# Attention's keys transposed four chunks at a time: 112-row tiles in place of 48-row pieces, and two weight buffers in place of three

## The chip, the cores and the metric

The kernel runs on one core of one Trainium2 chip. The metric is the device time of one execution in microseconds (us). A core has a matrix engine (PE, with its weight loads listed apart as PEld), three engines for elementwise work (DVE, ACT, POOL) and a queue engine (SP) that issues the DMAs. Each engine works through its own list of instructions in order. PE reads SBUF and writes PSUM, which has eight banks.

## What is computed

Three layers, one after the other, in fp32 (B = 4, H = 8, S = 768, D = 48; 3072 tokens of 384 channels):

```python
for t in range(S):                       # attention: a gated linear recurrence per head
    state = alpha[:, :, t, :, None] * state + np.einsum('bhd,bhe->bhde', k[:, :, t], v[:, :, t])
    y[:, :, t] = np.einsum('bhd,bhde->bhe', q[:, :, t], state)
...
P = np.exp(logits)                       # mixture of 8 experts: 8 rounds of row and column scaling
...
for e in range(E):
    out += P[:, e:e + 1] * (np.maximum(x @ w1[e], 0.0) @ w2[e])
...
h = x @ w_in                             # last layer
g = h * np.cos(h)
return (g @ w_out).astype(np.float32)
```

## The kernel before

**Matrix products.** Each fp32 operand of the large products is split into a high and a low part of type fp32r, and a product is made of three (high by high, high by low, low by high). The weights come in passes: 8 experts and 2 halves of the last layer. A pass has 8 weight pieces `w{c}{i}` (chunk c = 0 to 3; i = 0 into the hidden layer, i = 1 out of it), each with a high tile `w..h` and a low tile `w..l`. A piece is loaded into a staging buffer `raw`, cast on ACT into `w..h`, and POOL writes the remainder to `w..l`; only then may the buffer take the next load (`Weights.prep`, `Weights.load`). There are `NRAW` staging buffers. The tiles of one pass are overwritten for the next while the last block of the pass runs.

**Stage 1** holds attention and the first expert, side by side. The tokens are cut into 12 units of 256, and a unit's heads into 4 pairs, so attention has 48 slots (unit, pair). In a slot (`attention`, the loop over `slots`):

- `ew`, two slots ahead: scans and products on DVE, ACT and POOL that make the decayed q, k and the tile `k6` (the keys, decayed to the end of their chunk of 64 tokens). A pair's two heads lie in partitions 0 to 47 and 64 to 111.
- PE transposes `k6` chunk by chunk into PSUM bank 0, and ACT copies it to `kt`. Call this group kT. Per chunk it is one `transpose` for the head at 64 to 111 and one `matmul` with the identity for the head at 0 to 47; in the trace the matmul counts twice, so four chunks are 12 PE instructions `bank<-ident,acc` with 48 rows.
- PE multiplies keys and queries (`pg`, 48 rows by 64), and values with `kt` (`pk`, 64 rows by 48); DVE carries the state over the chunks; PE makes the output (`py`, 128 rows by 48) one slot later, and ACT copies it to `x`.

As soon as a unit's 4 pairs are done, the first expert's block of that unit can run (`Passes.block`): per hidden tile 9 products of `w.0` and 9 of `w.1`, all 128 rows by 128 columns with 256 tokens moving. These are called R below, the name of no tile. After attention, `sinkhorn` scales the gates, and stage 2 runs passes 1 to 9 in blocks of 512 tokens.

**What sets the order.** A `Plan` records all instructions and issues them by a list scheduler: every instruction has a rank (attention 0, products 1, `ew` and weight preparation 1 or 2), a planned cost and planned waits, and each engine takes the lowest rank among what is ready. The planned cost of a PE instruction with up to 64 columns differs from that of a wider one, so a change of shape changes the order.

**Memory.** `late` are the last 1024 columns of the output accumulator `acc`, unused until attention ends; `k6` (three tiles) and `qka` (q, k and alpha as loaded, four tiles) lie there and in `fbuf`.

Of the kernel before, what the change touches and what calls it, by code (L numbers as in the profile page):

```python
# [9 lines left out]
F32 = mybir.dt.float32  # L10
# [9 lines left out]
B, H, S, D = 4, 8, 768, 48  # L20
# [5 lines left out]
CH = 64  # L26
# [4 lines left out]
UN = 256  # L31
# [3 lines left out]
AMIN, AMAX = 0.25, 1.0  # L35
LAG = 2
LAG3 = 3
NRAW = 3
FARENA, RARENA = 9232, 10240
SEG = 32  # L40
SCAN = (SEG + 1) * (UN // SEG)
DBG = None
# [15 lines left out]
def vw(t, off, dims, p0=0, p1=128):  # L58
    a = t[p0:p1]
    return bass.AP(a.tensor, a.offset + off, [list(a.ap[0])] + [list(d) for d in dims])  # L60
# [130 lines left out]
class Arena:  # L191
# [17 lines left out]
    def ring(self, n, shape, dtype):  # L209
        return ring([self.tile(shape, dtype) for i in range(n)])  # L210
# [8 lines left out]
class Weights:  # L219
# [7 lines left out]
    def load(self):  # L227
        if self.loaded == len(self.order):
            return
        p, c, i = key = self.order[self.loaded]  # L230
        r = self.raw[key] = self.k.raw[self.loaded % NRAW]
        self.loaded += 1
# [79 lines left out]
class Kernel:  # L312
    def __init__(self, tc, ctx, qka, vv, nat, vt, wts, w8, wg, cst, out):
# [9 lines left out]
        self.w = [[[const.tile([128, CW], F32R, name=f"w{c}{i}{z}") for z in "hl"] for i in range(2)] for c in range(NCH)]  # L323
        self.raw = [const.tile([128, CW], F32, name=f"raw{i}") for i in range(NRAW)]
        self.ident = const.tile([128, 128], F32, name="ident")
# [61 lines left out]
    def attention(self, pool):  # L387
        e = self.e
        V, A, G, T, SP = e.vector, e.scalar, e.gpsimd, e.tensor, e.sync
        nt0 = UN // CH  # L390
# [9 lines left out]
        m1, m2 = tots()[:, 0:1], tots()[0:1, 0:1]  # L400

        late = [Arena(self.acc[:, k, NTOK - 4 * UN:]) for k in range(KT)]
        qka = ring([z.tile([128, 3, UN], F32) for z in late + [pool]])
        k6s, mask = ring([z.tile([128, UN], F32) for z in late]), self.mask
        pt0, pk = (self.bank[i][:, :nt0 * D].rearrange("p (t d) -> p t d", d=D) for i in (0, 2))
        pg0, py0 = (self.bank[i][:, :UN] for i in (1, 3))
        V.memset(pk, 0.0)
        V.memset(py0, 0.0)
# [10 lines left out]
        def load_v(ui):  # L419
            b, s0, n = UNITS[ui]  # L420
            t = vs[ui % 2]
            for h in range(2):
                r = slice(64 * h, 64 * h + 64)
                SP.dma_start(out=t[r, h], in_=self.vv[b, s0 // UN, r])

        def ew(i):
            t = loaded.pop(i)
            n = UNITS[slots[i][0]][2]
            X, k6, rp, tot, a, f = xt(), k6s(), rps(), tots(), decs(), fwds()
            self.rank(2)  # L430
            state[i] = dict(X=X, k6=k6, qk=t, tot=tot)
            nb, seg = n // 64, [[SEG + 1, n // SEG], [1, SEG]]
            flat = [[SEG, n // SEG], [1, SEG]]

            def tt(eng, o_, a_, b_):
                eng.tensor_tensor(out=o_, in0=a_, in1=b_, op=ALU.mult)

            V.tensor_scalar(vw(a, 1, seg), vw(t, 2 * UN, flat), AMIN, AMAX, op0=ALU.max, op1=ALU.min)

            V.tensor_tensor_scan(out=f[:, :SCAN], data0=a[:, :SCAN], data1=self.heads, initial=0.0, op0=ALU.mult, op1=ALU.add)  # L440
            V.tensor_tensor_scan(out=vw(bwd, SCAN, [[-1, SCAN]]), data0=vw(a, SCAN, [[-1, SCAN]]), data1=self.heads, initial=0.0, op0=ALU.mult, op1=ALU.add)
            tt(G, vw(t, 0, flat), vw(t, 0, flat), vw(f, 1, seg))
            tt(V, vw(t, UN, flat), vw(t, UN, flat), vw(bwd, 2, seg))
            G.tensor_tensor(out=vw(t, 2 * UN, flat), in0=vw(t, 2 * UN, flat), in1=vw(a, 1, seg), op=ALU.subtract)
            first, second = SEG, 2 * SEG + 1
            tt(V, tot[:, :nb], vw(f, first, [[2 * SEG + 2, nb]]), vw(f, second, [[2 * SEG + 2, nb]]))
            tt(V, vw(k6, 0, [[64, nb], [1, 32]]), vw(t, UN, [[64, nb], [1, 32]]), vw(f, second, [[2 * SEG + 2, nb], [0, 32]]))
            A.copy(vw(k6, 32, [[64, nb], [1, 32]]), vw(t, UN + 32, [[64, nb], [1, 32]]))
            V.reciprocal(rp[:, :n // SEG], vw(f, first, [[SEG + 1, n // SEG]]))
            for p0, h in ((0, 1), (64, 0)):  # L450
                p1 = p0 + 64
                tt(V, vw(X, h * UN + 32, [[64, nb], [1, 32]], p0, p1), vw(t, 32, [[64, nb], [1, 32]], p0, p1), vw(f, first, [[2 * SEG + 2, nb], [0, 32]], p0, p1))
                A.copy(vw(X, h * UN, [[64, nb], [1, 32]], p0, p1), vw(t, 0, [[64, nb], [1, 32]], p0, p1))
            a1 = vw(t, 0, [[UN + 32, 2], [64, nb], [1, 32]])
            tt(G, a1, a1, vw(rp, 0, [[1, 2], [2, nb], [0, 32]]))
# [23 lines left out]
        for i in range(len(slots) + 1):  # L479
            if i + 2 < len(slots):  # L480
                ew(i + 2)
            self.rank(0)
            if i < len(slots):
                ui, p = slots[i]
                b, s0, n = UNITS[ui]
                nt = n // CH
                if p == 0 and ui + 1 < len(UNITS):
                    load_v(ui + 1)
                st = state[i]
                t, k6, X, tot = st["qk"], st["k6"], st["X"], st["tot"]  # L490
                pt, pg, kt = pt0[:, :nt], pg0[:, :n], kts()[:, :nt]
                for j in range(nt):
                    T.transpose(pt[0:64, j], k6[64:112, j * CH:(j + 1) * CH], self.ident[64:112, 64:112])
                    T.matmul(pt[64:128, j], k6[0:48, j * CH:(j + 1) * CH], self.ident[0:48, 0:48], start=True, stop=True)
                A.copy(kt, pt)
                yield
                for j in range(nt):
                    js = slice(j * CH, (j + 1) * CH)
                    T.matmul(pg[0:64, js], t[64:112, 1, js], t[64:112, 0, js], start=True, stop=True)
                    T.matmul(pg[64:128, js], t[0:48, 1, js], t[0:48, 0, js], start=True, stop=True)  # L500
                V.copy_predicated(X[0:64, 0, :n], mask[0:64, :n], pg[0:64])
                V.copy_predicated(X[64:128, 1, :n], mask[64:128, :n], pg[64:128])

                self.rank(3)
                d = t[:, 2, :n]
                A.activation(d, d, AF.Square, accum_out=adev[:, i:i + 1])
                if i + 4 < len(slots):
                    loaded[i + 4] = load_qka(*slots[i + 4])
                yield
                self.rank(0)  # L510
                vt, so = vs[ui % 2], sc
                if s0 == 0:
                    G.memset(so[:, p, 0], 0.0)
                for j in range(nt):
                    T.matmul(pk[64:112, j], kt[0:64, j], vt[0:64, 0, p, j], start=True, stop=True)
                    T.matmul(pk[0:48, j], kt[64:128, j], vt[64:128, 1, p, j], start=True, stop=True)
                def step(j):
                    V.scalar_tensor_tensor(out=so[:, p, (j + 1) % nt], in0=so[:, p, j], scalar=tot[:, j:j + 1],
                                           in1=pk[:, j], op0=ALU.mult, op1=ALU.add)

                for j in range(nt - 1):
                    step(j)
                A.copy(vt[64:112, 0, p, :nt], so[64:112, p, :nt])
                A.copy(vt[0:48, 1, p, :nt], so[0:48, p, :nt])
                if s0 + n < S:
                    step(nt - 1)
                yield
            if i > 0:
                ui, p = slots[i - 1]
                b, s0, n = UNITS[ui]  # L530
                nt = n // CH
                X = state.pop(i - 1)["X"]
                vt = vs[ui % 2]
                py = py0[:, :n]
                for j in range(nt):
                    js = slice(j * CH, (j + 1) * CH)
                    T.matmul(py[64:112, js], vt[:, 0, p, j], X[:, 0, js], start=True, stop=True)
                    T.matmul(py[0:48, js], vt[:, 1, p, j], X[:, 1, js], start=True, stop=True)
                t0 = b * S + s0
                if p < 3:  # L540
                    A.copy(self.x[0:48, p, t0:t0 + n], py[0:48])
                    A.copy(self.x[64:112, p, t0:t0 + n], py[64:112])
                else:
                    yt = yts()[:, :n]
                    A.copy(yt, py)
                    self.pieces(yt, t0, n)
                if p == 2:
                    self.done = ui + 1
            yield
# [77 lines left out]
    def stage1(self):  # L627
# [22 lines left out]
        self.rank(2)  # L650
        for _ in range(NRAW):
            w.load()
# [106 lines left out]
    def general(self):  # L759
# [48 lines left out]
        w = self.wq = Weights(self, 0)  # L808
        for _ in range(NRAW):
            w.load()  # L810
# [79 lines left out]
```

## Time and profile before

| what | us |
|---|---|
| median of 3 runs | 2270.36 (2268.06 to 2280.47) |
| the profiled execution, its own time | 2266.68 |
| its span, first to last instruction | 2264.9 |
| PE busy in the span | 2221.3 (98%) |
| DVE, POOL, ACT busy | 1074.9, 815.5, 773.9 |

The profiled execution is 3.7 us under the median, and 1.8 us of its time lie outside the span. PE's busy time is a union of instructions that overlap (a new one starts before the last has drained), so a full PE can still be given less to do; what an instruction costs is read from the distance between starts, not from its duration.

### The profile page before, as it was taken

Reading aid. Unit: us, or ns where it says so; the run is one execution under the profiler, and the core shown is the slowest. Engines: PE = TensorE matmul, PEld = TensorE weight load, DVE = VectorE, ACT = ScalarE, POOL = GpSimd, SP = SyncE. Lnnn points to the kernel's source line nnn. Section 1 sums busy time; section 2 is a strip of 40 time slices with the busy share of each in tenths; the row PEclk is TensorE's granted clock in tenths of the full one; section 3 lists DMA queues with packets and bytes.
Section 4 is the critical chain, followed back from the end, with each engine's and each line's share of the span. In section 5 each row is a group of like instructions: output and inputs, shape, how many; then the busy total and the mean of one; then the engine's idle time right before and its main releaser. Section 6 shows DMA issues by size and latency. Waiting matters only on the chain. (4 is left out here: it accounts for less than half of the span.)

```text
span 2264.9 us, 32287 instructions
## 1 busy us (share of the span) xinstructions
PE 2221.3 (98%) x12790; PEld 1878.9 (83%) x12790; DVE 1074.9 (47%) x2113; ACT 773.9 (34%) x1628; POOL 815.5 (36%) x688
## 2 busy tenths in 40 slices
PE   5999999999999999999999999999999999999998
PEld 4888888978888888888888888888888889998997
DVE  7767667532222333334233423423342237777675
ACT  3444444421122122112212221221222136667664
POOL 5334333243342234224223422422342255447442
PEclk9999999999999999999999999999999999999999
DMA  4211211020011112102111211211120010000000
GB/s 140 80 60 59 68 60 60 10 74 19 19 49 45 31 39 65 29 25 60 47 31 39 65 29 25 61 46 31 40 65 17 5 42 15 1 8 29 29 29 30
DMA packets 70705, 94.89 MB, mean 42 GB/s; under 512 B 6992, under 2 KB 52624, under 8 KB 70544
## 3 DMA queue, kind: packets, MB, share of 16 engines
q1 hardware_dynamic: 70544, 92.74, 13.7%
q8 instruction: 102, 1.67, 0.3%
q14 instruction: 59, 0.48, 0.1%
HBM read 80.42 MB, written 11.11 MB: 40 GB/s over the span
## 5 line engine op out<-in xcount | busy, mean ns | idle before, releaser
L180 DVE SCALAR_TENSOR_TENSOR rbuf<-bank,rbuf 128x512 fp32r<-128x512 f32 (+1 forms) x432 | 271.1, 629 | 822.5 <-ACT rbuf L180 821.6
L180 ACT ACTIVATE rbuf<-bank 128x512 fp32r<-128x512 f32 (+1 forms) x432 | 237.0, 549 | 1021.8 <-PE bank L180 1021.2
L180 POOL TENSOR_TENSOR rbuf<-x,rbuf 128x512 fp32r<-128x512 f32 (+1 forms) x162 | 187.2, 1178 | 716.4 <-ACT rbuf L180 695.8
L180 POOL TENSOR_TENSOR acc<-acc,fbuf 128x512 f32<-128x512 f32 (+1 forms) x252 | 268.4, 1087 | 329.7 <-DVE fbuf L180 239.6
L180 PE MATMUL bank<-rbuf,w11h 128*128 128x512 f32 (+1 forms) x648 | 203.5, 371 | 0.9 <-ACT fbuf L180 0.5
L180 PE MATMUL bank<-rbuf,w21h 128*128 128x512 f32 (+1 forms) x648 | 202.5, 371 | 0.0
L180 PE MATMUL bank<-rbuf,w01h 128*128 128x512 f32 (+1 forms) x648 | 201.2, 370 | 0.3 <-ACT acc L180 0.3
L180 PE MATMUL bank<-rbuf,w31h 128*128 128x512 f32 (+1 forms) x648 | 201.3, 370 | 0.0
L180 POOL TENSOR_TENSOR rbuf<-fbuf,rbuf 128x512 fp32r<-128x512 f32 x96 | 128.2, 1335 | 192.9 <-ACT rbuf L180 186.0
L180 PE MATMUL bank<-rbuf,w00h 128*128 128x512 f32 (+1 forms) x792 | 192.0, 376 | 2.3 <-ACT rbuf L180 2.1
L180 PE MATMUL bank<-rbuf,w10h 128*128 128x512 f32 (+1 forms) x792 | 192.7, 375 | 0.1
L180 DVE TENSOR_SCALAR fbuf<-fbuf 128x192 uint32<-128x192 uint32 (+3 forms) x252 | 151.2, 621 | 85.8 <-ACT fbuf L180 85.1
L180 PE MATMUL bank<-rbuf,w20h 128*128 128x512 f32 (+1 forms) x792 | 191.5, 375 | 0.0
L180 PE MATMUL bank<-rbuf,w30h 128*128 128x512 f32 (+1 forms) x792 | 191.2, 374 | 0.3 <-ACT w30h L180 0.3
L180 DVE SCALAR_TENSOR_TENSOR fbuf<-fbuf 128x192 uint32<-128x192 uint32 (+2 forms) x288 | 176.6, 613 | 6.0
L180 PEld LDWEIGHTS bank<-rbuf,w00h 128*128 128x128 f32 x792 | 141.8, 190 | 28.4 <-ACT rbuf L180 2.6
L180 PEld LDWEIGHTS bank<-rbuf,w30h 128*128 128x128 f32 x792 | 140.8, 188 | 26.5 <-ACT w30h L180 0.7
L180 PEld LDWEIGHTS bank<-rbuf,w10h 128*128 128x128 f32 x792 | 140.5, 188 | 25.7 <-DVE fbuf L180 0.9
L180 PEld LDWEIGHTS bank<-rbuf,w20h 128*128 128x128 f32 x792 | 141.0, 189 | 25.0
L180 ACT ACTIVATE fbuf<-fbuf 128x512 f32<-128x512 f32 (+1 forms) x204 | 135.0, 662 | 51.2 <-DVE fbuf L180 49.5
L180 DVE TENSOR_TENSOR fbuf<-bank,fbuf 128x512 f32<-128x512 f32 x126 | 82.8, 684 | 136.7 <-PE bank L180 136.6
L180 DVE SCALAR_TENSOR_TENSOR fbuf<-fbuf,bank 128x48 f32<-128x48 f32 (+1 forms) x272 | 111.5, 410 | 56.2 <-PE bank L180 32.0
(119 smaller groups left out, 3892.6 us busy)
## 6 DMA issues: line engine op xcount, KB each, us to landing
raw<-in_wts_dram SPq DMA_DIRECT2D x64, 384.0 KB, 3.1
acc<-in_qka_dram SPq DMA_DIRECT2D x36, 384.0 KB, 3.1
fbuf<-pt SPq DMA_DIRECT2D x48, 256.0 KB, 4.8
fbuf<-in_w_dram SPq DMA_DIRECT2D x64, 192.0 KB, 2.6
w<-fbuf SPq DMA_DIRECT2D x64, 96.0 KB, 1.6
raw<-w SPq DMA_DIRECT2D x16, 384.0 KB, 3.0
fbuf<-in_vv_dram SPq DMA_DIRECT2D x24, 192.0 KB, 3.2
fbuf<-in_qka_dram SPq DMA_DIRECT2D x12, 384.0 KB, 3.9
```

The costliest lines, as they stand in the source:

```text
L180: getattr(getattr(self.nc, eng), name)(*args, **kw)
```

## The change

Each chunk's transpose now takes partitions 0 to 111 of `k6` (both heads, and the unused rows between) and two chunks of columns (128), so that one instruction brings chunk j of one head to partitions 0 to 63 and chunk j + 1 of the other head to 64 to 127. Four transposes do for a slot. For the last one `k6` is 64 columns longer and ACT copies the first chunk behind the last. The copy from PSUM to `kt` becomes two, one for each half of the partitions, and the `pk` products take the second head's chunk from slot j - 1 of `kt`. The wider `k6` tiles all lie in `late[0]`, two of the four `qka` tiles lie in `fbuf`, and the space comes from one staging buffer for weights: three become two.

```diff
-NRAW = 3
-FARENA, RARENA = 9232, 10240
+NRAW = 2
+FARENA, RARENA = 10000, 10240
...
-        qka = ring([z.tile([128, 3, UN], F32) for z in late + [pool]])
-        k6s, mask = ring([z.tile([128, UN], F32) for z in late]), self.mask
-        pt0, pk = (self.bank[i][:, :nt0 * D].rearrange("p (t d) -> p t d", d=D) for i in (0, 2))
+
+        k6s, mask = late[0].ring(3, [128, UN + CH], F32), self.mask
+        qka = ring([z.tile([128, 3, UN], F32) for z in late[1:] + [pool, pool]])
+        pt0 = self.bank[0][:, :nt0 * 112].rearrange("p (t d) -> p t d", d=112)
+        pk = self.bank[2][:, :nt0 * D].rearrange("p (t d) -> p t d", d=D)
...
             A.copy(vw(k6, 32, [[64, nb], [1, 32]]), vw(t, UN + 32, [[64, nb], [1, 32]]))
+            A.copy(k6[0:112, n:n + CH], k6[0:112, 0:CH])
...
                 for j in range(nt):
-                    T.transpose(pt[0:64, j], k6[64:112, j * CH:(j + 1) * CH], self.ident[64:112, 64:112])
-                    T.matmul(pt[64:128, j], k6[0:48, j * CH:(j + 1) * CH], self.ident[0:48, 0:48], start=True, stop=True)
-                A.copy(kt, pt)
+                    T.transpose(pt[:, j], k6[0:112, j * CH:(j + 2) * CH], self.ident[0:112, 0:112])
+                A.copy(kt[0:64], pt[0:64, :, 64:112])
+                A.copy(kt[64:128], pt[64:128, :, 0:48])
...
-                    T.matmul(pk[0:48, j], kt[64:128, j], vt[64:128, 1, p, j], start=True, stop=True)
+                    T.matmul(pk[0:48, j], kt[64:128, (j - 1) % nt], vt[64:128, 1, p, j], start=True, stop=True)
```

The change also moves instructions, since the scheduler plans the new shapes and buffers differently. PE, a place in stage 1 where the first unit's products run between attention's groups, before the change (a row is a run of like instructions; the last column counts them, and a matmul counts once here):

```order
L180 MATMUL bank_97<-rbuf,w00h 128x256
L180 MATMUL bank_97<-rbuf,w00l 128x256 x2
L180 MATMUL bank_93<-ident,acc 64x48 x8
L180 MATMUL bank_97<-rbuf,w00l 128x256
L180 MATMUL bank_98<-rbuf,w00h 128x256
L180 MATMUL bank_98<-rbuf,w00l 128x256
L180 MATMUL bank_94<-acc 64x64 x8
```

And a place in the same first unit after it:

```order
L180 MATMUL bank_98<-rbuf,w01l 128x256
L180 MATMUL bank_98<-rbuf,w01h 128x256
L180 MATMUL bank_92<-ident,acc 128x112 x3
L180 MATMUL bank_99<-rbuf,w01h 128x256
L180 MATMUL bank_99<-rbuf,w01l 128x256
L180 MATMUL bank_93<-acc 64x64 x8
L180 MATMUL bank_99<-rbuf,w01h 128x256
L180 MATMUL bank_92<-ident,acc 128x112
L180 MATMUL bank_98<-rbuf,w11h 128x256
```

The eight 64-by-48 pieces are four of 128 by 112, and here the four are parted by other work. Over all 48 slots kT stands in 49 runs before and 66 after. Counted on PE's list from the 12th slot's `py` to the 48th's, there were 1212 R and are 1056; up to the 48th slot's `py` 1476 before and 1272 after, so that 204 more of the first expert's products stand behind attention.

ACT, where pass 1 ends and the weights of pass 2 are cast (`CAST w..h<-raw`), between the activations that read PSUM (`rbuf<-bank`), before:

```order
L180 CAST w21h<-raw_74 128x768
L180 CAST w20h<-raw_76 128x768
L180 ACTIVATE rbuf<-bank_94 128x512
L180 ACTIVATE rbuf<-bank_100 128x512
L180 CAST w30h<-raw_75 128x768
L180 ACTIVATE rbuf<-bank_93 128x512
L180 ACTIVATE rbuf<-bank_94 128x512
L180 ACTIVATE rbuf<-bank_100 128x512
L180 ACTIVATE rbuf<-bank_93 128x512
L180 CAST w31h<-raw_76 128x768
```

The same place after the change:

```order
L180 CAST w20h<-raw_74 128x768
L180 ACTIVATE rbuf<-bank_92 128x512
L180 ACTIVATE rbuf<-bank_93 128x512
L180 CAST w21h<-raw_75 128x768
L180 ACTIVATE rbuf<-bank_99 128x512
L180 CAST w30h<-raw_74 128x768
L180 ACTIVATE rbuf<-bank_99 128x512
L180 ACTIVATE rbuf<-bank_92 128x512
L180 CAST rbuf<-x 128x512
L180 ACTIVATE rbuf<-bank_93 128x512
L180 CAST rbuf<-x 128x512 x2
L180 CAST w31h<-raw_75 128x768
```

The casts follow each other by buffer, raw_74 and raw_75 in turn, and the last one stands two activations later on ACT's list, behind the casts of the next block's tokens. On PE's list the first use of w31h of pass 2 stood 37 products behind the one that the activation ahead of its cast reads, and now 18 behind.

## Rows read from the trace of the kernel before

**Rows 1.** The page: the span, and each engine's busy us, share and instructions.

```profile
span 2264.9 us, 32287 instructions
...
PE 2221.3 (98%) x12790; PEld 1878.9 (83%) x12790; DVE 1074.9 (47%) x2113; ACT 773.9 (34%) x1628; POOL 815.5 (36%) x688
```

**Rows 2.** Busy time by stretch: PE, PEld, DVE, ACT, POOL, granted clock, DMA share.

```profile
0.00:57.00 57.00, 30.95 (x282) 24.52 (x282) 41.44 (x97) 21.06 (x59) 31.60 (x40) 1.00 0.46 141
57.00:114.00 57.00, 56.81 (x628) 48.52 (x628) 40.09 (x113) 25.96 (x88) 21.95 (x29) 1.00 0.24 77
114.00:400.00 286.00, 284.27 (x3231) 247.41 (x3231) 199.40 (x577) 138.11 (x460) 100.34 (x138) 0.98 0.20 61
400.00:500.00 100.00, 92.95 (x717) 82.96 (x717) 46.79 (x123) 36.30 (x92) 35.50 (x28) 1.00 0.16 44
500.00:2264.90 1764.90, 1756.28 (x7936) 1475.50 (x7934) 747.22 (x1206) 552.48 (x931) 626.11 (x454) 1.00 0.12 34
```

**Rows 3.** Groups by shape, PE from 57 to 409 us: busy, mean ns, idle before.

```profile
L180 PE MATMUL bank<-ident,acc 48*64 48x48 f32 x516 | 73.6, 237 | 1.4 <-DVE acc L180 1.4
```

**Rows 4.** PE in order of time, 210.5 to 213.3 us: start, length, instructions.

```profile
210.72 0.40 PE L180 MATMUL bank<-rbuf,w31h 128*128 128x256 f32 x2
210.96 0.28 PE L180 MATMUL bank<-rbuf,w31l 128*128 128x256 f32 x1
211.16 1.68 PE L180 MATMUL bank<-ident,acc 48*64 48x48 f32 x12
212.77 0.39 PE L180 MATMUL bank<-rbuf,w31h 128*128 128x256 f32 x1
213.00 0.51 PE L180 MATMUL bank<-rbuf,w10h 128*128 128x256 f32 x3
```

**Rows 5.** PE in order of time, 182 to 193 us.

```profile
182.44 0.56 PE L180 MATMUL bank<-fbuf 64*48 64x48 f32 x16
182.93 0.50 PE L180 MATMUL bank<-rbuf,w11h 128*128 128x256 f32 x2
```

**Rows 6.** PE in order of time, 472.2 to 473.5 us: a transpose in sinkhorn's last step.

```profile
472.71 0.27 PE L180 MATMUL bank<-ident,P 128*128 128x128 f32 x1
472.74 0.48 PE L180 MATMUL bank<-rbuf,w10l 128*128 128x512 f32 x1
473.05 0.40 PE L180 MATMUL bank<-rbuf,w01h 128*128 128x512 f32 x1
473.29 0.40 PE L180 MATMUL bank<-rbuf,w01l 128*128 128x512 f32 x1
```

**Rows 7.** PE in order of time, 437.3 to 438.4 us: a plain fp32 product.

```profile
437.16 0.75 PE L180 MATMUL bank<-rbuf,w30h 128*128 128x256 f32 x5
437.75 0.49 PE L180 MATMUL bank<-P,ones 128*128 128x192 f32 x2
437.94 0.42 PE L180 MATMUL bank<-rbuf,w30h 128*128 128x256 f32 x1
438.20 0.40 PE L180 MATMUL bank<-rbuf,w30l 128*128 128x256 f32 x2
```

**Rows 8.** Groups by shape, DVE and ACT, 114 to 400 us.

```profile
L180 DVE SCALAR_TENSOR_TENSOR rbuf<-bank,rbuf 128x256 fp32r<-128x256 f32 x63 | 26.0, 417 | 33.2 <-ACT rbuf L180 32.8 <-PE bank L180 0.2
...
L180 ACT COPY fbuf<-bank 128x192 f32<-128x192 f32 x34 | 10.8, 319 | 48.5 <-PE bank L180 48.5
...
L180 ACT COPY acc<-acc 128x128 f32<-128x128 f32 x27 | 8.0, 298 | 0.5
```

**Rows 9.** The waits, 114 to 400 us: who waited for whom, total, times, longest.

```profile
DVE fbuf L180 <- PE bank L180: 38.5, 32, 4.1
DVE rbuf L180 <- ACT rbuf L180: 32.8, 23, 3.3
```

**Rows 10.** The tile raw, 440 to 2264 us: ns min, median, max.

```profile
L180 ACT CAST w31h<-raw x9: 817/828/839, 499.0 to 2074.7; 128x768 fp32r<-128x768 f32 x9
L180 POOL TENSOR_TENSOR w31l<-raw,w31h x9: 1849/1849/2036, 501.4 to 2079.0; 128x768 fp32r<-128x768 f32 x9
...
DMA to landing us min/median/max: 2.7/3.0/9.0
```

## The prediction

> **What bounds the kernel now.** I read the page first: PE is busy for 98% of the span, no other engine for half of it [rows 1]. That share is an average, so the next view was the busy time by stretch [rows 2]. From 500 us on PE is full and DVE stands at 42%; the change touches nothing there but the staging of weights. From 57 to 400 us, the stretch of attention beside the first expert, PE is full too (341 of 343 us) while DVE has 70%, ACT 48%, POOL 35%. Before 57 us PE is busy for 31 us only: there the first slots go at the pace of DVE, ACT and the loads. So the question is how much of PE's time the transposes take between 57 us and the end of attention, and what comes next when it is gone.
>
> The groups by shape give kT 516 records in that stretch [rows 3], which at 12 a slot are 43 slots. Their busy time of 73.6 us hides what they cost beside products that overlap with them. In order of time [rows 4] one R starts 0.12 us after the other; the R at 210.96 is followed by kT, and the second R after kT starts at 213.00. That is 2.04 us for two R (0.24) and one kT, so **one kT costs 1.80 us** of PE, some 77 us over 43 slots. A piece takes 1.61 / 12 = 0.134 us, where the 16 pieces of a pk group, of much the same shape, take 0.49 us, 0.03 each [rows 5]: it is the turn from transpose to plain matmul and back that is paid for, eight times in a slot, as well as entering and leaving.
>
> **What the new transposes cost.** No row shows a transpose of 112 rows. The nearest is one of 128 by 128 in fp32 between two R of 512 tokens [rows 6]: it starts at 472.71, the R behind it at 472.74, the R behind that at 473.05, and an R of that size takes 0.24 us (473.05 to 473.29). So it took 0.34 - 0.24 = 0.10 us all told, with no price for entering or leaving. It uses the array's full width, as R does. Lower bound: 112 of 128 columns move, 0.09 us. Upper bound: a plain fp32 pass of 192 columns, 0.45 us for two from 437.75 to 438.20 less one R, 0.165 us each [rows 7]. I take 0.10, the row of the same operation; four are 0.40 us, bounds 0.36 to 0.66. Between two R a slot's kT then falls by 1.4 us. Not all stand so: the list of PE has 66 runs of kT, and part of them border on pg, pk or py, where the array has to change its division once more than it would for R alone. I take 1.3 us a slot: 43 x 1.3 = **56 us less of PE's work**, bounds 43 x 1.05 = 45 and 43 x 1.4 = 60.
>
> The Trainium skill, "TensorE: Matmul & The Clock Gate", section "Part 4: PE-mode transpose", speaks against so low a price: about 275 ns for one 128 by 128 transpose in a kernel, bf16. By it four would be an estimated 1.1 us and the 56 us would be 26. The trace agrees on the length of a record and not on the cost, as its row of fp32 shows; the rival "one after the other" below has its own numbers.
>
> **What is added.** ACT: the copy of the first chunk (64 columns; a copy of 128 columns takes 0.30 us) and a second copy out of PSUM in place of one of 0.32 us [rows 8], at most 0.6 us a slot on an engine with 48% [rows 2]; hidden, unless ACT is what PE waits for. If bare, 43 x 0.6 = 26 us. The wait of kT for its first copy is covered by `ew` running two slots ahead.
>
> **What comes next.** 34.6 slots lie in 286 us, 8.27 us each. After the change a slot holds 1.3 us less of kT and 4.4 R less (1212 and 1056 over 36 slots), 0.5 us, so PE asks for 6.45 us. DVE has 199.4 / 34.6 = 5.77 us a slot now, less 4.4 / 18 activations' worth of its 0.42 us [rows 8], so 5.67: 88% of the new slot. DVE also waits 38.5 us for PE and 32.8 for ACT's activations behind PE [rows 9], 2.1 us a slot, and only 0.8 us will be left. A faster PE shortens these waits but not all, and PE's list is in order, so what stands behind a late pg, pk or py waits too. No row shows how dense DVE can run here. Bounds: it fits (0), or it stays at the 73% that it had in the first 57 us, where PE was not what held it (a slot of 7.8 us, which gives back 1.3 us and so all of the gain). I take 0.35 us a slot (DVE at 83%): 43 x 0.35 = **15 us given back**.
>
> The 204 R that now stand behind attention are 24 us of PE work, done later and neither saved nor lost. They lie beside sinkhorn, where PE idles for 7 us of the 100 [rows 2]; up to that may be gained, and I count nothing.
>
> **First 57 us.** kT there is work of an engine that idles for 26 us; four slots' chains lose a little on PE and gain a copy or two on ACT. The casts of chunks 1 to 3 stand later on ACT's list, since only two buffers turn, but attention's own groups are there to run. I take 2 us of gain, bounds -4 to +6.
>
> **Two staging buffers.** One turn of a buffer is a cast, 0.83 us, a subtraction, 1.85, and a load, 3.0 from issue to landing [rows 10], 5.7 us. Eight pieces need three reloads on the way from two buffers and two from three, at each of 9 changes of pass. What hides it: a piece is cast only when the last block has let go of its old tile, some 8 us apart (two of eight hidden tiles, 36 R of 0.23). On PE's list the closest pair still has 18 R, 4.2 us, between the activation ahead of the cast and the first use, against 0.6 + 0.83 + 1.85 us of activation, cast and subtraction. At the change from pass 0 to 1 the blocks are half as long and a load took up to 9.0 us [rows 10]; there I take **3 us lost**, bounds 0 and 15; elsewhere nothing.
>
> **The sum.** -56 + 15 - 2 + 3 = -40 us against the profiled execution's own 2266.7: **2227 us**. The median of the runs shown is 3.7 us higher, so a median after may well be some us above it; 0.5% of it, about what can be told from no change, is 11 us.
>
> **Rivals.**
> - *All of it.* Slots are dense at once, 60 us saved, 2 at the start, the 7 idle us beside sinkhorn filled, nothing lost: 2267 - 69 = 2198. For it: DVE's waits are mostly on PE. Against: 88% of an engine in strict order. Chance 0.17.
> - *DVE becomes the bound* at 80%: a slot of 7.1 us, which gives back 0.65 a slot: 56 - 28 + 2 - 3 = 27 saved, 2240. For it: no stretch shows DVE above 73%. Against: it was never pressed. With waits on PE the granted clock, 0.98 in this stretch [rows 2], could fall more often, which costs the same way. Chance 0.15, from here down to 2252.
> - *One after the other.* The transposes follow each other at their recorded length of 0.27 us [rows 6], 1.08 for four: 1.80 - 1.08 - 0.1 for neighbours is 0.62 a slot, 27 us; slots of 7.1 us leave DVE at 80%, so little is given back, 5 us; with the start and pass 1, 27 - 5 + 2 - 3 = 21: 2246. For it: four weight loads of 128 columns in a row, each for one short product, and no row of two full transposes in a row. Against: the 0.10 us above. It would take the skill's figure. Chance 0.08.
> - *Slower: the weights come late.* If nothing hides the third reload, each of 9 changes of pass waits 5.7 us: 51 us, so 2227 + 51 = 2278, slower by 0.5%. From 4.4 us a change the gain is gone. For it: the margin of w31 shrank from 37 to 18 R. Against: all that is said under staging. Chance 0.03.
> - *No gain:* DVE and ACT at their present density, as in the bound above: 2262 to 2267. Chance 0.05.
>
> My forecast, 2210 to 2237, keeps 0.52. The range reaches to the full gain and to the foot of the second and third rivals: 2198 to 2252. Faster by over 0.5% are all cases but the last two, 0.92; the same 0.05; slower 0.03.
>
> **What would show it.** In the profile after: kT in 4 records a slot, and between two R the time of four transposes near 0.4 us (right), or 0.7 to 1.1 (third rival). A slot between 57 and 400 us at 6.5 to 6.9 us, PE with some idle time ended by DVE or ACT, DVE at 80% or more. Sinkhorn's transposes some 40 to 60 us earlier than 472. From there to the end the length unchanged within 5 us, and no wait of PE for `w..h` or `w..l` above 1 us; many of them would be the fourth rival. Wrong at the root would be a PE that is full as before with the same span.

## The result, and the profile after

| | before, in the same runs | after |
|---|---|---|
| median of 4 runs, us | 2272.11 (2268.06 to 2280.47) | 2240.39 (2238.62 to 2242.62) |
| ratio | | 0.9863, 95% [0.9843, 0.9882] |
| the profiled execution, its own time; its span | 2266.68; 2264.9 | 2242.62; 2240.7 |

Faster by 1.4%: 2240 lies in the range of 2198 to 2252 and 13 us above the forecast of 2227. The sum was made against the profiled execution, and there the change saves 24 us where 40 were forecast (between the two medians it is 32).

The page of the kernel after:

```profile
span 2240.7 us, 31634 instructions
...
PE 2176.2 (97%) x12406; PEld 1848.9 (83%) x12406; DVE 1092.9 (49%) x2113; ACT 797.3 (36%) x1724; POOL 818.3 (37%) x688
```

PE has 384 instructions less, 8 for each of 48 slots, and its share fell from 98% [rows 1] to 97%: PE now waits somewhere. The busy time by stretch of the kernel after shows where (PE, PEld, DVE, ACT, POOL, granted clock, DMA share). The second row is the whole of attention beside the first expert; the others are stretches of [rows 2] that the next paragraphs use.

```profile
0.00:57.00 57.00, 35.72 (x359) 30.09 (x359) 47.05 (x114) 27.56 (x84) 33.26 (x44) 1.00 0.43 131
...
57.00:340.00 283.00, 266.46 (x3332) 237.68 (x3331) 248.64 (x678) 180.62 (x622) 126.67 (x167) 0.99 0.26 78
...
400.00:500.00 100.00, 99.56 (x492) 82.90 (x491) 20.57 (x33) 24.97 (x46) 48.80 (x35) 1.00 0.20 55
500.00:2240.70 1740.70, 1714.46 (x7698) 1439.80 (x7696) 744.94 (x1187) 543.43 (x915) 602.86 (x436) 0.99 0.12 34
```

From 57 to 340 us PE idles for 16.5 us, where before it idled for 1.9 from 57 to 400, and DVE is busy for 248.6 of 283 us, 88%. Some idle time of PE and a dense DVE were forecast (DVE at 83%). Not forecast is the last row: PE idles for 26 us behind 500 us, where before it idled for 9.

To see what each stretch gained, I compare landmarks that stand in the same place of the program in both: sinkhorn's last transpose, and the cast of `w00h` for each pass, which comes with the first block of hidden work that lets go of the old tile. The tile ident, from 440 us of the kernel before; the first and last start stand ahead of the shapes:

```profile
L180 PE MATMUL bank<-ident,P x2: 271/272/272, 472.7 to 474.4; 128*128 128x128 f32 x1, 128*64 128x128 f32 x1
```

The same of the kernel after, and below it its tile raw, from 1755 and from 1790 us:

```profile
L180 PE MATMUL bank<-ident,P x2: 270/270/271, 395.8 to 397.4; 128*128 128x128 f32 x1, 128*64 128x128 f32 x1
...
L180 ACT CAST w00h<-raw x1: 828/828/828, 1770.1 to 1770.1; 128x768 fp32r<-128x768 f32 x1
...
L180 ACT CAST w00h<-raw x1: 818/818/818, 1982.5 to 1982.5; 128x768 fp32r<-128x768 f32 x1
```

And the tile raw of the kernel before at the same two casts:

```profile
L180 ACT CAST w00h<-raw x1: 824/824/824, 1824.5 to 1824.5; 128x768 fp32r<-128x768 f32 x1
...
L180 ACT CAST w00h<-raw x9: 818/827/858, 447.3 to 2024.6; 128x768 fp32r<-128x768 f32 x9
```

Sinkhorn ends 77 us earlier, with some 24 us of the first expert's products left for later, as the change's own rows said. At the cast for pass 8 the changed kernel is 54.4 us ahead (1824.5 and 1770.1). From there to the cast for pass 9 it takes 212.4 us where before took 200.1, and from that to the end 258.2 us where before took 240.3. So **54 us were gained in stage 1 and 30 lost where passes 7 and 8 end**, where the last layer's weights come in.

What PE waited for after stage 1, in the kernel after (who waited for whom: total, times, longest):

```profile
PE bank L180 <- ACT rbuf L180: 11.9, 4, 5.3
PE bank L180 <- DVE fbuf L180: 7.1, 3, 3.4
```

No wait for a weight tile or a load is there. PE waits for the cosine chain of the last layer's hidden tiles, the steps that make `h * np.cos(h)`. In order of time, all engines, 1817 to 1826 us, the steps of one hidden tile and PE's last products before its wait; then PE alone, 17 us later:

```profile
1817.84 0.60 ACT L180 ACTIVATE fbuf<-bank 128x512 f32<-128x512 f32 x1 [2.52 <-PE bank L180]
...
1818.47 0.43 DVE L180 TENSOR_SCALAR fbuf<-fbuf 128x512 f32<-128x512 f32 x1 [3.81 <-ACT fbuf L180]
...
1819.00 0.69 DVE L180 SCALAR_TENSOR_TENSOR fbuf<-fbuf,bank 128x512 f32<-128x512 f32 x1
...
1819.72 1.91 DVE L180 SCALAR_TENSOR_TENSOR fbuf<-fbuf 128x512 f32<-128x512 f32 x1
...
1820.45 0.87 PE L180 MATMUL bank<-w11h,rbuf 128*128 128x384 f32 x4
...
1821.73 1.38 ACT L180 ACTIVATE fbuf<-fbuf 128x512 f32<-128x512 f32 x2 [2.07 <-DVE fbuf L180]
...
1823.41 0.68 DVE L180 TENSOR_TENSOR fbuf<-fbuf,bank 128x512 f32<-128x512 f32 x1
...
1824.87 0.60 ACT L180 CAST rbuf<-fbuf 128x512 fp32r<-128x512 f32 x1
...
1825.53 0.69 PE L180 MATMUL bank<-w21h,rbuf 128*128 128x384 f32 x1 [4.21 <-ACT rbuf L180]
```

```profile
1842.27 2.93 PE L180 MATMUL bank<-rbuf,w10h 128*128 128x512 f32 x6 [3.40 <-DVE fbuf L180]
```

From the tile's first activation at 1817.84 to the product that reads its result at 1825.53 the chain takes 7.7 us: ACT, three steps on DVE, two on ACT, one more on DVE, and ACT's cast, with steps of the next tile between them. (The DVE step at 1819.72 took 1.91 us where the next tile's took 0.69, at 1822.80; POOL's subtraction for `w21l` ran beside it, from 1819.23 to 1821.08. Whether one lengthens the other was not tested.) PE has no product to put into the last 4.2 us. The second wait, 3.4 us, ends on DVE, whose last step of a chain is also the last to read the PSUM bank that the next hidden tile's products write. How many products cover such a chain I counted in PE's order: in the first block of pass 8 the second product of a hidden tile stands [46, 58, 61, 64, 64, 64, 64, 64] products behind its first before, and [46, 55, 55, 55, 34, 50, 41, 58] after; in pass 9 after [64, 55, 39, 49, 28, 35, 50, 60]. The granted clock costs something besides. Windows of the kernel after, PE alone (PE busy, granted clock, DMA share and GB/s):

```profile
1811.00:1815.00 4.00, 4.00 (x23) 1.00 0.00 0
...
1819.00:1823.00 4.00, 2.32 (x14) 1.00 0.19 57
1823.00:1827.00 4.00, 1.47 (x5) 0.69 0.10 41
1827.00:1831.00 4.00, 4.00 (x13) 0.50 0.07 11
1831.00:1835.00 4.00, 4.00 (x19) 0.95 0.28 91
...
1811.00:1850.00 39.00, 31.39 (x128) 0.82 0.13 41
...
2003.00:2065.00 62.00, 50.98 (x223) 0.88 0.09 29
```

The clock falls to the lower of its two levels, 0.50, at the end of the wait of 4.2 us and is back some 6 us after PE's products have resumed. Idle time in the last two rows is 7.6 + 11.0 = 18.6 us; the clock costs an estimated 0.18 x 31.4 + 0.12 x 51.0 = 11.8 us more: 30.4 together, close to the loss of 30 us.

### The profile page after: what moved, and what is told of

It reads as the page before. It is cut to its first block, busy times and chain, and to the rows that moved or that the text cites. A ratio compares the mean times of both kernels' runs of the same rounds, so it can differ in the third digit from the quotient of the medians.

```text
span 2240.7 us, 31634 instructions
## 1 busy us (share of the span) xinstructions
PE 2176.2 (97%) x12406; PEld 1848.9 (83%) x12406; DVE 1092.9 (49%) x2113; ACT 797.3 (36%) x1724; POOL 818.3 (37%) x688
## 4 chain that ended last, share of the span: by engine, by line
PE 88%; DVE 9%; ACT 2%; issue 1%; DMA 0%; SPq 0%; POOL 0%; DVEq 0%; ACTq 0%; POOLq 0%
PE bank L180 88%; DVE fbuf L180 7%; ACT fbuf L180 1%; DVE acc L180 1%; DVE rbuf L180 1%; ACT rbuf L180 0%; DMA fbuf<-in_cst_dram 0%; DVE x L180 0%; ACT x L180 0%; ACT acc L180 0%; SPq L180 0%; DVE Lg L180 0%; POOL rbuf L180 0%; DVEq L180 0%; ACTq L180 0%
## 5 line engine op out<-in xcount | busy, mean ns | idle before, releaser
L180 POOL TENSOR_TENSOR acc<-acc,fbuf 128x512 f32<-128x512 f32 (+1 forms) x216 | 241.6, 1142 | 283.2 <-DVE fbuf L180 228.8
L180 PE MATMUL bank<-rbuf,w21h 128*128 128x512 f32 (+1 forms) x648 | 201.6, 368 | 0.0
L180 DVE TENSOR_SCALAR fbuf<-fbuf 128x192 uint32<-128x192 uint32 (+4 forms) x264 | 150.3, 589 | 104.1 <-ACT fbuf L180 103.3
L180 DVE SCALAR_TENSOR_TENSOR fbuf<-fbuf 128x192 uint32<-128x192 uint32 (+2 forms) x288 | 188.3, 654 | 6.1
L180 ACT ACTIVATE fbuf<-fbuf 128x512 f32<-128x512 f32 (+1 forms) x216 | 139.9, 648 | 54.9 <-DVE fbuf L180 52.7
L180 PEld LDWEIGHTS bank<-rbuf,w11h 128*128 128x128 f32 x648 | 119.1, 189 | 21.0 <-ACT rbuf L180 0.7
```

The lines of the kernel that those rows point to most:

```text
L180: getattr(getattr(self.nc, eng), name)(*args, **kw)
```

## The experiments

The questions: are the 30 us due to two staging buffers, to the new transposes or to the planned order; where do 54 us of gain come from; and does DVE bound stage 1 now? Each kernel was timed four times, the kernel before beside it.

**Three buffers in the changed kernel.** Some small tiles move into unused parts of `late` and of sinkhorn's scratch, which makes room for the third buffer.

```diff
-NRAW = 2
-FARENA, RARENA = 10000, 10240
+NRAW = 3
+FARENA, RARENA = 9524, 10240
...
```

> The changed kernel with three staging buffers again; the room comes from small tiles moved into the unused columns of the late arenas and from P and ones moved into the scratch of sinkhorn. The trace after shows 30 us lost at the last two changes of pass. Theory A (two buffers, planned with the planner's margins, put the casts so late on ACT's list that PE's list brings a hidden tile's second product within 28 to 41 R of its first, where it had 64, and the chain of the cosine is exposed): 64 again, no wait there, 2208 to 2214 us. Rival B (two buffers are too few in fact: loads land late): 2208 to 2214 as well. Rival C (the moved buffers or attention's new order cost the time, not the count of staging buffers): 2236 to 2244. Stage 1 as after: kT 0.4 us between two R.

2237.09 us (2235.72 to 2237.29), ratio 0.9858 [0.9829, 0.9886]: next to no gain over the 2240.39, a time in the range of rival C. But the waits at the last two changes are gone: from cast to cast of `w00h` 1791.4 to 1993.0, 201.6 us, and 240.9 to the end. The kernel lost it elsewhere: the cast for pass 8 came 21 us later than in the kernel after. The windows of 900 us within passes 1 to 7, PE alone, of the kernel after and then of this one:

```profile
700.00:1600.00 900.00, 900.00 (x3933) 1.00 0.15 42
```

```profile
700.00:1600.00 900.00, 900.00 (x3859) 1.00 0.14 40
```

PE is full and at full clock in both, and yet 74 products fewer fit: 900 / 3933 = 0.2288 us each, and 900 / 3859 = 0.2332. One thing that had changed for these products is where `rbuf` starts: the arena in front of it is 9524 elements long, 38096 bytes, 16 above a multiple of 64 (counted from the tiles' sizes; the trace holds no addresses). That asked for two more runs, below.

**Two buffers in the kernel before.**

```diff
-NRAW = 3
+NRAW = 2
```

> The kernel before with two staging buffers and nothing else changed. Theory A and rival B: the two waits come back at the changes from pass 7 to 8 and from 8 to 9, 12 and 18 us, and stage 1 loses little: 2295 to 2305 us. Rival C: 2266 to 2275.

2295.48 us (2291.99 to 2302.74), ratio 1.0110 [1.0079, 1.0140]: slower by 1.1%. Its casts stand 212.1 us apart and 258.7 us lie behind the second, as in the kernel after (212.4 and 258.2), and PE's order of time has the same two waits:

```profile
1885.44 0.69 PE L180 MATMUL bank<-w21h,rbuf 128*128 128x384 f32 x1 [4.26 <-ACT rbuf L180]
1902.07 2.93 PE L180 MATMUL bank<-rbuf,w10h 128*128 128x512 f32 x6 [3.41 <-DVE fbuf L180]
```

The products between a hidden tile's first and second number [46, 55, 55, 55, 34, 50, 41, 58] in the first block of pass 8, the same as in the kernel after. So the loss comes with the second half of the change, the buffers, and needs none of the first.

**Two buffers without the planner's margin.** The planner keeps an instruction of a rank above 0 that waits for another engine back for 2.5 us more (4 us on SP; none on PE). With two buffers that delay is paid at every turn of a buffer. Here it is taken from those steps alone.

```diff
+    def staged(self, i):
+        args, kw = self.ops[i][2:4]
+        return any(isinstance(a, bass.AP) and a.tensor.name.startswith("raw") for a in [*args, *kw.values()])
...
+                if self.staged(i) and self.staged(u):
+                    late = 0
```

> The changed kernel with its two buffers; the planner alone is told another thing: between two instructions that touch a staging buffer its extra margins of 2.5 and 4.0 us are left out, so it places casts, subtractions and loads earlier on their lists. Theory A: PE's list has 64 R between first and second product again, and the 30 us are gone: 2208 to 2216 us. Rival B: the loads are late in fact, PE now waits for w..h or w..l at all nine changes of pass: 2240 us or more. Rival C: 2236 to 2244.

2210.19 us (2208.29 to 2211.63), ratio 0.9736 [0.9707, 0.9766]. The casts are at 1770.1 and 1968.7, 198.6 us apart, and 240.9 us lie behind. PE alone in the stretches where the kernel after had waited:

```profile
1790.00:1850.00 60.00, 60.00 (x290) 1.00 0.11 34
...
2003.00:2065.00 62.00, 61.44 (x311) 1.00 0.08 26
```

All 30 us are back with two buffers and the same loads. So the transfers were never too slow: it is the order that the planner writes when it believes the casts late. Between a hidden tile's first and second product stand [46, 58, 61, 64, 64, 64, 64, 64] again, as before the change.

**The turns alone.** In the kernel before, the four transposes of a slot stand together and then the four identity matmuls, so the array turns between the two once inside a slot and not seven times. Nothing else changes.

```diff
                 for j in range(nt):
                     T.transpose(pt[0:64, j], k6[64:112, j * CH:(j + 1) * CH], self.ident[64:112, 64:112])
+                for j in range(nt):
                     T.matmul(pt[64:128, j], k6[0:48, j * CH:(j + 1) * CH], self.ident[0:48, 0:48], start=True, stop=True)
```

> The kernel before with one line more: the four transposes of a slot first, then its four products with the identity, so that PE turns from transpose to plain product once and not four times. Same instructions, same operands. If the turns are what kT pays for: steps of 0.09 us inside a kind in place of 0.15 to 0.16, kT about 1.4 us in place of 1.80, 43 x 0.4 = 17 us, 2250 to 2258 us. Rival: the narrow pieces cost 0.134 us each whatever stands beside them: 2266 to 2275. Third: they fall to the 0.03 us of the pk pieces: 2215 to 2225.

2229.68 us (2229.38 to 2230.24), ratio 0.9825 [0.9796, 0.9854]: with one added line and three buffers, this is faster than the change as made. It lies in none of the three ranges: the turns cost about twice what was expected (kT 1.07 us, not 1.4). PE in order of time, beside [rows 4] the same twelve instructions:

```profile
195.08 0.28 PE L180 MATMUL bank<-rbuf,w31l 128*128 128x256 f32 x1
195.29 0.95 PE L180 MATMUL bank<-ident,acc 48*64 48x48 f32 x12
196.17 0.38 PE L180 MATMUL bank<-rbuf,w31h 128*128 128x256 f32 x1
196.39 0.87 PE L180 MATMUL bank<-rbuf,w10h 128*128 128x256 f32 x6
```

From 195.08 to 196.39 are two R and one kT: 1.31 - 0.24 = 1.07 us, against 1.80 before. All groups that stand whole between two R, 25 in either trace, have a median of 1.08 here and 1.81 before. Turning cost 0.73 us a slot, some 0.12 for each of the six turns less; 43 slots make 31 us of the 40 that this kernel saves, and the rest was not taken apart. Two things change at each turn: transpose against plain product, and the partitions, since the transposes read 64 to 111 and write 0 to 63 where the products read 0 to 47 and write 64 to 127. The pk pieces change sides in the same way from one product to the next (they read 0 to 63 and 64 to 127 in turn) and take 0.03 us each [rows 5], so that change alone is not what costs; what remains is transpose against product. The Trainium skill, "TensorEngine Tiling (Array Packing)", section "Key Properties", says that a change of tiling mode drains the array, and that a change of tile alone does not count as one. The pk pieces agree (0.03 us); whether the tiling mode changes between these transposes and products, no row shows.

**Where the tokens start.** First the third buffer again, with an arena whose end lies at a multiple of 64 bytes (the diff is against the run with three buffers above); then the kernel without margin, with a flag of 16 bytes put ahead of `rbuf`.

```diff
-FARENA, RARENA = 9524, 10240
+FARENA, RARENA = 9552, 10240
```

> The version with three staging buffers and moved small tiles, but fbuf 28 columns longer (9552 for 9524), so that everything behind it starts at the byte at which it starts before and after the change (a multiple of 64; it had been 16 above one). With 9524 the products of passes 1 to 7 followed each other every 233.3 ns where they take 228.9, which lost 24 us. If the starting byte does that: 228.9 ns again, 2207 to 2215 us. If the moved tiles or the third buffer do it: 2233 to 2240.

```diff
+        self.flag = const.tile([1, 4], I32, name="flag")[:, 0:1]
...
-        self.flag = const.tile([1, 1], I32, name="flag")
```

> Two buffers without the planner's margins (2210 us), and one flag tile of 16 bytes put ahead of rbuf, so that rbuf, mask, x and acc start 16 bytes later; no instruction moves. If the starting byte costs 4.4 ns a product of 512 columns in passes 1 to 7, some 6050 of them: 24 to 27 us more, 2232 to 2240. If it does not: 2207 to 2214.

Aligned: 2207.01 us (2206.46 to 2207.77), ratio 0.9732 [0.9716, 0.9748], 30 us under the same kernel with an arena 112 bytes shorter, and the fastest of all that compute the whole reference. Shifted: 2240.71 us (2240.24 to 2241.62), ratio 0.9883 [0.9866, 0.9899], 30.5 us over the same kernel without the shift. The 900 us of passes 1 to 7 in the shifted kernel hold 3859 instructions of PE, in the aligned one 3933. In either pair, with and without the 16 bytes, the traces have the same instructions of PE in the same order from first to last, so that the order is not what costs. Sinkhorn ends alike in the shifted kernel and its twin (400.5 and 401.3 us), and from there to the cast for pass 8 it takes 1395.0 us where the twin takes 1368.8. So 26 us of the 30.5 are lost ahead of the cast for pass 8.

**Is DVE next in stage 1?** Three changes to the kernel without margin: the planner is told 96 ns for a transpose of 112 rows, as measured, in place of 220; one product of `ew` goes from DVE to POOL; the same product is left out.

```diff
+            if name == "transpose" and n == 112:
+                return 96
```

> Two buffers without margins, and the planner's cost of a new transpose is 96 ns, as measured, where its rule made it 220. PE's list then holds 1445 R up to the end of attention, not 1302, in line with PE's real pace. If PE's waits in attention come from a list planned for a slower PE: 3 to 8 us gained, 2202 to 2207. If they come from DVE, which stands at 85%: no gain, or up to 5 us lost since attention is spread wider, 2208 to 2216.

```diff
-            tt(V, vw(t, UN, flat), vw(t, UN, flat), vw(bwd, 2, seg))
+            tt(G, vw(t, UN, flat), vw(t, UN, flat), vw(bwd, 2, seg))
```

> Two buffers without margins, and the product of the keys with the backward decay, 128 by 256, 0.46 us of DVE in every slot, is POOL's. If DVE is what stage 1 waits for now: 48 x 0.46 = 22 us of DVE's work gone, PE's 15 us of waits about halved, 2200 to 2206. Rival: the product takes 0.8 us on POOL and stands in the chain that makes k6, so PE waits for that in place of DVE: 2210 to 2220.

```diff
-            tt(V, vw(t, UN, flat), vw(t, UN, flat), vw(bwd, 2, seg))
```

> Two buffers without margins (2210 us), and the product of the keys with the backward decay is left out altogether, so attention's values are not those of the reference: 0.46 us of DVE a slot go, and nothing takes their place. If DVE is what PE still waits for in attention (about 15 us of idle PE): 2200 to 2205 us. If DVE's load is not the cause, and PE waits for single chains that its list meets too early: 2208 to 2213.

The planned cost gains nothing: 2212.02 us (2211.80 to 2212.97), as expected if DVE is what PE waits for. The product on POOL costs 39 us: 2249.65 (2247.57 to 2251.19), outside both ranges. The product left out gives 2198.40 us (2197.39 to 2199.91), 11.8 less and a little below the range for DVE. From 57 to 340 us, the kernel without margin and then the one without the product:

```profile
57.00:340.00 283.00, 271.58 (x3367) 243.91 (x3366) 237.45 (x680) 179.30 (x617) 122.78 (x166) 0.99 0.24 73
```

```profile
57.00:340.00 283.00, 279.45 (x3559) 252.63 (x3559) 228.55 (x657) 187.78 (x643) 123.22 (x168) 1.00 0.24 74
```

With 8.9 us less of DVE's work in the window PE's idle time falls from 11.4 to 3.6 us, and it gets through 192 instructions more. Leaving the product out also reorders PE's list; but the planned cost reordered it too and gained nothing, so DVE is what PE waits for in this stage. To move the work is another matter: with the product on POOL attention's groups are spread longer over PE's list (1433 R up to the last kT, where the kernel without margin has 1206), and there is a stretch where PE has gaps (PE 56.8 of 70 us, granted clock 0.76):

```profile
330.00:400.00 70.00, 56.81 (x642) 49.97 (x641) 45.77 (x130) 35.85 (x121) 26.36 (x40) 0.76 0.14 44
```

The 13.2 us of gaps and an estimated 0.24 x 56.8 = 13.6 us of clock are 27 of the 39; where the others are was not taken apart.

**Both repairs.** Three aligned buffers, and no margin on staging.

> Three staging buffers at the old starting byte, and no planner's margins at the staging buffers. If the margins cost something with three buffers too (PE's order at each change of pass): 2203 to 2206 us. If all of their cost lay in the two last changes with two buffers: 2206 to 2209, as with margins.

2218.49 us (2215.16 to 2221.49), ratio 0.9763 [0.9728, 0.9799], slower than with either repair and outside both ranges. Behind the cast for pass 8 nothing is lost (198.6 and 240.8 us); the 14 us more of its span than with three aligned buffers alone are there by the cast for pass 8, at 1780.3 against 1766.5. From 57 to 340 us PE idles for 13.4 us here and for 8.1 there, and the granted clock is 0.96 here and 0.99 there: 5.3 us, and an estimated 0.03 x 270 = 8 us, which is most of the 14. The lists of stage 1 differ, and which of the differences brings these waits was not taken apart.

## Why the prediction was right, and where it was wrong

**kT between two R: right.** Forecast 0.40 us, bounds 0.36 to 0.66. PE in order of time, kernel after:

```profile
326.30 0.28 PE L180 MATMUL bank<-rbuf,w31h 128*128 128x256 f32 x1
326.42 0.55 PE L180 MATMUL bank<-ident,acc 112*128 112x112 f32 x4
326.73 0.36 PE L180 MATMUL bank<-rbuf,w31l 128*128 128x256 f32 x1
326.93 0.39 PE L180 MATMUL bank<-rbuf,w31h 128*128 128x256 f32 x2
```

From 326.30 to 326.93 are 0.63 us for two R (0.24) and four transposes: 0.39 by the reckoning that gave 1.80 before, 0.10 each. Of the 12 groups that stand whole between two R, seven read 0.40 to 0.41, one 0.47, and four hold a gap besides. The rival *One after the other*, at 1.08, is out. The Trainium skill's 275 ns ("TensorE: Matmul & The Clock Gate", "Part 4: PE-mode transpose") is again near the length of a record, whose median here is 259 ns, and not the price between products. The turns were the right reason for about half of the old price: grouped, kT still costs 1.07 us, so 0.73 us of the 1.4 that the new transposes save are turns, and the rest comes from fewer and wider pieces.

**What comes next: the slot right, and partly by luck.** From the first transpose of the ninth slot to that of the 48th the kernel before takes 407.4 - 83.6 = 323.8 us, 8.30 a slot, and the one after 338.1 - 72.1 = 266.0, 6.82 a slot, where 6.45 + 0.35 = 6.80 was forecast. PE's idle time between 57 us and attention's end grew by 14.6 us; 15 were to be given back. These same 39 slots, before and then after:

```profile
83.60:407.40 323.80, 320.51 (x3677) 278.26 (x3676) 224.43 (x650) 155.13 (x519) 113.17 (x158) 0.98 0.20 61
```

```profile
72.10:338.10 266.00, 252.41 (x3147) 225.29 (x3148) 235.33 (x640) 170.34 (x586) 120.91 (x160) 0.99 0.25 76
```

DVE's work was 5.75 us a slot and is 6.03, where 5.67 was forecast: with ten instructions less it is busy for 11 us more, because some of its products take longer (`acc<-acc,fbuf` of 128 by 256 has a mean of 466 ns before and 590 after; why was not tested). DVE runs denser than forecast, at 88% and not 83%. The two errors cancel: 6.03 at 88% and 5.67 at 83% make the same slot. The waits of PE from 57 to 340 us, kernel after:

```profile
PE bank L180 <- DVE rbuf L180: 7.9, 12, 2.4
...
PE bank L180 <- DVE fbuf L180: 6.0, 7, 2.8
...
DVE fbuf L180 <- PE bank L180: 13.4, 15, 1.6
```

14 of the 16.5 idle us end on DVE, and DVE's own waits for PE fell to 13.4 us from 38.5 [rows 9]. *DVE becomes the bound* was right as to the engine, and too dear: DVE runs at 88% from 57 to 340 us, not at 80. ACT's added copies are hidden but for some 2 us.

**Stage 1 as a whole: 54 us against 43.** PE's idle time sorts it, from [rows 2] and the windows after. First 57 us: 26.0 and 21.3, a gain of 4.8 where 2 was forecast. From 57 us to 400 (before) and to 340 (after): 14.6 lost. 400 to 500 us, and 340 to 500 after: 7.05 and 0.4, a gain of 6.6, the idle time beside sinkhorn of which I had counted nothing. What is left of 54.4 is 57.6 us, by subtraction: kT itself with whatever else changed in PE's work and clock, 1.2 for each of 48 slots, where 56 was forecast for 43. So two small terms were too small: the start, and the 204 R that came to stand beside sinkhorn and filled it. The 3 us lost from pass 0 to 1 did not occur: PE idles for 0.4 us from 340 to 500, where that change lies (the cast of `w00h` for pass 1 starts at 401.1), and not at all from 500 to 1811. Two of the signs named in advance failed: sinkhorn's transposes came 77 us earlier, not 40 to 60, and from there to the end it takes 1843 us where before took 1790, not the same within 5. Both had left out the 24 us of moved products that the prediction itself names; the other 30 are the next point.

**Two staging buffers, "elsewhere nothing": wrong.** That is the step that failed: 30 us were lost at two of the nine changes. I had asked whether the weights come in time, found 18 R against 3.3 us of activation, cast and subtraction, and concluded that nothing waits. The weights did come in time; no wait for them is in the trace. What I did not follow is what the list does instead: the planner adds its margin to each turn of a buffer, so it thinks the casts later than they are, and fills the wait by bringing a hidden tile's second product forward. In passes 2 to 7 the distances fall too (from 37 to 21 at the closest; in pass 1 from 19 to 10), but behind a hidden tile stand only an activation and one step on DVE there, and PE has no wait. In passes 8 and 9 it is the cosine chain, 7.7 us at the wait shown. The margin of one row of the list, in pass 2, was taken for all nine changes, though the last layer's activation is another one. The rival *Slower: the weights come late* had the place, the changes of pass, and the wrong mechanism; its price of 5.7 us a change was 12 and 18 us at two of them and nothing at the others.

**The size of the total.** 40 forecast, 24 measured in the profiled execution: +11 from stage 1, +3 from pass 1, -30 from the two changes of pass. That the total lies in the range owes something to luck: the range was drawn for other reasons than this loss, and the gain in stage 1 that had not been counted hides a part of it.

## What to carry to other kernels

A buffer taken away is not only a question of whether loads keep up: where a planner writes the order, look at what it does with the later times that it now assumes, and check the distance between a producer and its reader in each kind of stage, the one with the longest chain of activations above all. Before a transposed layout is rebuilt, try grouping like instructions: one line here gave 40 us, more than the 32 of the whole change as made, because each turn between transpose and product cost some 0.12 us. When tiles move, look at where the large operands start. And a sum that comes out right is checked term by term: here DVE's work and its density were both off and cancelled.

## What was not expected of the hardware

A start of `rbuf` and the tiles behind it 16 bytes above a multiple of 64 (by the tiles' sizes) makes products of 512 columns follow each other every 233.2 ns in place of 228.8, with PE full at a granted clock of 1.00 in both. It was shown in both directions, on two kernels, and is worth 30 us of 2200. In passes 8 and 9 the price is smaller (200.7 us from cast to cast in the shifted kernel, 198.6 in its twin), and their two kinds of product show why: those of 512 columns, which move tokens out of `rbuf` past a weight tile, go from a mean of 229.7 to 233.4 ns between starts, while those of 384 columns, which move a weight tile past a tile of `rbuf`, go from 174.3 to 175.1 (three buffers, the other pair: 229.6 and 231.9, 174.3 and 175.2). So most of the price goes with moving an operand out of the shifted tile. Other offsets were not tried, and how far `x` and `acc` move with the flag is not known.
